# A DeltaNet attention and MLP kernel: from a scheduler's order to one written order with the MLP in small units

## The chip, the core and the metric

The kernel runs on one core of a Trainium2 chip. Its time is the device time of one execution in microseconds (us). TensorE (PE) multiplies, VectorE (DVE), ScalarE (ACT) and GpSimd (POOL) work elementwise, SyncE (SP) and ACT issue DMAs. Each engine runs its own instructions in order and waits on semaphores for the others.

## The reference

The output of a DeltaNet attention (batch 4, 8 heads, 768 tokens, head size 48) goes through an MLP 384 -> 2048 -> 384 with hardswish. q, k, v, beta are fp32; the two MLP weights arrive as float64 (a standard normal divided by a float64 number) and the kernel works in fp32.

```python
def _attn_ref(q, k, v, beta):
    B, H, S, D = q.shape                       # 4, 8, 768, 48
    k_n = k / (np.linalg.norm(k, axis=-1, keepdims=True) + 1e-06)
    state = np.zeros((B, H, D, D), dtype=np.float32)
    for t in range(S):
        kt, vt, bt = (k_n[:, :, t], v[:, :, t], beta[:, :, t, None])
        y[:, :, t] = np.einsum('bhd,bhde->bhe', q[:, :, t], state)
        v_old = np.einsum('bhde,bhd->bhe', state, kt)
        state = state + bt[:, :, :, None] * np.einsum('bhd,bhe->bhde', kt, vt - v_old)
    return y

def _moe_ref(x, w_in, w_out):                  # x: 3072 x 384
    h = x @ w_in
    return ((h * np.clip(h + 3.0, 0.0, 6.0) / 6.0) @ w_out).astype(np.float32)
```

## The kernel before

The 768 tokens are cut into 24 chunks of 32; a chunk's 32 tokens of all 4 batches fill the 128 partitions. Four chunks make a group, two chunks a block of the MLP (12 blocks of 256 tokens).

**Per group**, `norms` (the reciprocal lengths of k: ACT squares, a DVE reduction and Newton steps) and `inverse` (a unit triangular 32x32 system per head, batch and chunk, inverted by 30 columns of two DVE operations each, `pr` L310 and `A` L314). The matrix goes through DRAM for that: `l_dram<-LB`, `A<-l_dram` (L302), the columns, `x_dram<-A`, `LB<-x_dram` (L326).

**Per chunk**, `prep` (GpSimd: `kb`, `mb`, `bkb`; TensorE: eight transposes `pt` and the scores `sc`; ACT: `KQ`; DVE: `LB`) and `chain`, the recurrence. Its steps on TensorE are `ks` (L352, state times k), `pz` (LB times R), `py` (a part of the state, L352, and a part of the heads, L362), `su` (L406, the update of the state) and `yt` (L424, transposes of y for the MLP). ks, both parts of py, pz and su are 32 calls each on parts of the array of 32 or 64 rows; an fp32 call is two records in the trace, so 64. Between them DVE makes `R` after ks and updates `state` after su, ACT makes `Z` after pz and `y` after py.

**Per block**, `mlp_block`: 16 groups of three `ph` calls (L438, 128x256) with `t` on ACT and `g` on DVE, then two chunks of 16 `po` calls (L455, 128x384), then `o` and the store.

**Weights.** `convert` turns the float64 words into fp32 in 24 pieces of w_in (128x256) and 16 of w_out (128x384): two masks `e` and `m`, a Relu on ACT, then three joining operations, five of the six on DVE. Raw pieces share the tag "d" with three buffers.

**Order.** For the first part (chunks 0 and 1) DVE and SP run in written order, the other engines are ordered by the scheduler; from chunk 2 on the scheduler orders everything. The source gives two chains, then an MLP block. What stands on TensorE is the small matmuls of a chunk with a few ph among them, and then a long run of ph and po. All q, k, v loads, weight loads, A, LB and the stores are issued on SP; `l_dram` and `x_dram` on ACT. PSUM has three buffers of two banks (psC) and two of one bank (psM).

Of the kernel before, what the change touches and what calls it, by code (L numbers as in the profile page):

```python
# [17 lines left out]
def kernel(  # L18
# [20 lines left out]
    nc = tc.nc  # L39
# [18 lines left out]
    stage = ctx.enter_context(tc.tile_pool(name="stage", bufs=4))  # L58
# [4 lines left out]
    psC = ctx.enter_context(tc.tile_pool(name="psC", bufs=3, space=PSUM))  # L63
    psM = ctx.enter_context(tc.tile_pool(name="psM", bufs=2, space=PSUM))
# [14 lines left out]
    def load_k(g):  # L79
        if g * GS < N:  # L80
            kfs[g] = stage.tile([P, GS, H, D], FP32, name="kf", bufs=2)
            for i in range(GS):
                for b in range(B):
                    nc.sync.dma_start(out=kfs[g][rows(b), i], in_=tokens(k, b, g * GS + i))
# [12 lines left out]
    beta_hm = stage.tile([P, S], FP32, name="beta_hm", tag="d", bufs=3)  # L97
# [3 lines left out]
    for t in qbufs + kbufs + bkbufs:  # L101
        nc.vector.memset(t[:, :, D:DP], 0.0)
# [6 lines left out]
    for j, value in enumerate((1.0, -1.0)):  # L109
# [25 lines left out]
    WP = 256  # L135
    weights = [
        (w_in[:, s, f : f + WP], moe_w_in[s * 128 : (s + 1) * 128, f : f + WP])
        for f in range(0, FF, WP) for s in range(NKT)
    ] + [
        (w_out[:, f, :], moe_w_out[f * 128 : (f + 1) * 128, :]) for f in range(NFC)  # L140
    ]
    NW = len(weights)
    raws, parts = {}, {}

    def load_w(i):
        if i >= NW:
            return
        dst, src = weights[i]
        if src.dtype == FP32:
            nc.sync.dma_start(out=dst, in_=src)  # L150
            return
        raws[i] = stage.tile([128, dst.shape[1], 2], U32, name="d", tag="d", bufs=3)
        nc.sync.dma_start(
            out=raws[i][:].rearrange("p f z -> p (f z)"), in_=src.bitcast(U32)
        )

    def split_w(i):
        if i not in raws:
            return
        hi, n = raws[i][:, :, 1], raws[i].shape[1]  # L160
        m = stage.tile([128, n], U32, name="m", bufs=2)
        e = stage.tile([128, n], U32, name="e", bufs=2)
        nc.vector.tensor_single_scalar(e[:], hi, 0x7FF00000, op=ALU.bitwise_and)  # L163
# [3 lines left out]
        nc.vector.tensor_scalar(  # L167
            out=m[:], in0=hi, scalar1=0x000FFFFF, scalar2=0x00100000,
            op0=ALU.bitwise_and, op1=ALU.bitwise_or,
        )  # L170
        parts[i] = m, e

    def join_w(i):
        if i not in parts:
            return
        (m, e), d = parts.pop(i), raws.pop(i)
        hi, lo = d[:, :, 1], d[:, :, 0]
        nc.vector.scalar_tensor_tensor(  # L178
            out=e[:], in0=hi, scalar=0x80000000, in1=e[:],
            op0=ALU.bitwise_and, op1=ALU.bitwise_or,  # L180
        )
        mf = m[:].bitcast(FP32)
        nc.vector.scalar_tensor_tensor(  # L183
            out=mf, in0=lo, scalar=2.0**-32, in1=m[:], op0=ALU.mult, op1=ALU.add
        )
        nc.vector.scalar_tensor_tensor(  # L186
            out=weights[i][0], in0=mf, scalar=2.0**-20, in1=e[:].bitcast(FP32),
            op0=ALU.mult, op1=ALU.mult,
        )

    def convert():

        for i in range(3):
            load_w(i)
        split_w(0)
        for i in range(NW):
            split_w(i + 1)
            join_w(i)
            load_w(i + 3)
            yield  # L200

# [3 lines left out]
    def norms(g):  # L205

        kf = kfs[g]
        ss = small.tile([P, GS, H], FP32, name="ss")
        for i in range(GS):
            sq = work.tile([P, H, D], FP32, name="sq", bufs=1)  # L210
            nc.scalar.activation(out=sq[:], in_=kf[:, i], func=ACTF.Square)
            nc.vector.tensor_reduce(out=ss[:, i, :], in_=sq[:], axis=AX.X, op=ALU.add)
        seed = small.tile([P, GS, H], U32, name="seed")
# [5 lines left out]
        for _ in range(4):  # L219
            t = small.tile([P, GS, H], FP32, name="nt")  # L220
# [4 lines left out]
            rn = small.tile([P, GS, H], FP32, name="nr")  # L225
# [4 lines left out]
        t = small.tile([P, GS, H], FP32, name="nt")  # L230
# [4 lines left out]
        inv = small.tile([P, GS, H], FP32, name="inv")  # L235
        nc.vector.reciprocal(out=inv[:], in_=t[:])
        invs[g] = inv
# [5 lines left out]
    def prep(t):  # L243
# [4 lines left out]
            in1=invs[g][:, i, :].unsqueeze(2).to_broadcast([P, H, D]), op=ALU.mult,  # L248
# [13 lines left out]
        )  # L262
        KQ = work.tile([128, NP, 2, P], FP32, name="KQ", bufs=7)
        pt = psC.tile([128, 2, NP, P], FP32, name="pt", tag="pc")
        for j, src in enumerate((kb, qb)):
            for p in range(NP):
                nc.tensor.transpose(  # L267
                    pt[:, j, p, :], src[:, 2 * p : 2 * p + 2].rearrange("p e w -> p (e w)"), ident[:]
                )
            nc.scalar.activation(out=KQ[:, :, j, :], in_=pt[:, j], func=ACTF.Copy)  # L270
        load_q(t + NQB)
        yield
# [11 lines left out]
        LB = work.tile([P, 2, NP, 2, C], FP32, name="LB", bufs=7)  # L284
# [7 lines left out]
        nc.scalar.dma_start(  # L292
# [6 lines left out]
    def inverse(g):  # L299

        A = work.tile([128, C, C], FP32, name="A", bufs=1)
        nc.sync.dma_start(  # L302
            out=A[:].rearrange("p c i -> p (c i)"),
            in_=l_dram[g][:].rearrange("t h (b c) i -> (t h b) (c i)", b=B),
        )
        for j in range(1, C - 1):
# [13 lines left out]
        nc.scalar.dma_start(  # L320
# [20 lines left out]
    def chain(t):  # L341
        KQ, LB = KQs.pop(t), LBs.pop(t)
# [40 lines left out]
        pz = banks("pz")  # L383
        of_heads(
            lambda h, b: pz[rows(b), 0, D * h : D * h + D], lambda h: LBv[:, he(h), 0, :], R, True
        )
        Zt = work.tile([P, DM], FP32, name="Z")
        nc.scalar.activation(out=Zt[:], in_=pz[:, 0, 0:DM], func=ACTF.Copy)
# [9 lines left out]
        y = work.tile([P, DM], FP32, name="y")  # L398
        nc.scalar.activation(out=by_pair(y[:]), in_=pairs(py), func=ACTF.Copy)
        if t < N - 1:  # L400
# [11 lines left out]
            for i in range(B // 2):  # L412
# [6 lines left out]
        blk, cc = divmod(t, CB)
        if cc == 0:  # L420
            xTs[blk] = mlp.tile([128, NKT, TB], FP32, name="xT", bufs=2)
        pt = banks("yt")[:, 0, :]
        for s in range(NKT):
            nc.tensor.transpose(pt[:, s * P : (s + 1) * P], y[:, s * 128 : (s + 1) * 128], ident[:])  # L424
        nc.vector.tensor_copy(
            out=xTs[blk][:, :, cc * P : (cc + 1) * P],
            in_=pt[:, 0 : NKT * P].rearrange("p (s w) -> p s w", s=NKT),
        )
        yield


    def mlp_block(blk):
        xT = xTs.pop(blk)
        gs = []
        for f in range(NFC):
# [14 lines left out]
            gs.append(g)  # L450
            yield
        for c in range(CB):
            po = psM.tile([128, DM], FP32, name="po", tag="pm")
            for f in range(NFC):
                nc.tensor.matmul(  # L455
# [114 lines left out]
```

## Time and profile before

| | |
|---|---|
| runs, us | 896.68, 890.95, 896.49; median 896.49 |
| profiled execution | 888.49 us; span of its profile 886.7 us |
| mean granted clock of TensorE | 0.941 |
| busy share | TensorE 80%, DVE 41%, ACT 21%, GpSimd 10% |
| last matmul ends, span ends | 882.4 us, 886.7 us |
| mean DVE time | g 0.42, state 0.55, R 0.55, LB 0.69 us |

The span runs from the first to the last instruction; the time of an execution is a little longer. Everything below is of the one profiled execution. Where a row of the trace says "issue", the engine waited for nothing that the profile shows. Half clock is a granted clock of 0.50.

### The profile page before, as it was taken

Reading aid. Unit: us, or ns where it says so; the run is one execution under the profiler, and the core shown is the slowest. Engines: PE = TensorE matmul, PEld = TensorE weight load, DVE = VectorE, ACT = ScalarE, POOL = GpSimd, SP = SyncE. Lnnn points to the kernel's source line nnn. Section 1 sums busy time; section 2 is a strip of 40 time slices with the busy share of each in tenths; the row PEclk is TensorE's granted clock in tenths of the full one; section 3 lists DMA queues with packets and bytes.
Section 4 is the critical chain, followed back from the end, with each engine's and each line's share of the span. In section 5 each row is a group of like instructions: output and inputs, shape, how many; then the busy total and the mean of one; then the engine's idle time right before and its main releaser. Section 6 shows DMA issues by size and latency. Waiting matters only on the chain.

```text
span 886.7 us, 25143 instructions
## 1 busy us (share of the span) xinstructions
PE 709.5 (80%) x11208; PEld 510.7 (58%) x11208; DVE 365.2 (41%) x1014; ACT 188.2 (21%) x377; POOL 86.1 (10%) x118
## 2 busy tenths in 40 slices
PE   2400047987889799799799898998898999999998
PEld 1200035753666576676676675766765757757674
DVE  4647598659528430266220373311391302212030
ACT  2310233421321121230121220211311302213030
POOL 4200032006130000300001300002000000000000
PEclk9999995987989899899799899899999998999999
DMA  5462526433432401333102214001204001000000
GB/s 111 106 149 49 108 56 168 100 102 99 82 59 66 78 1 24 59 78 60 28 0 44 47 35 76 12 9 27 54 4 76 8 9 23 1 20 1 10 9 19
DMA packets 140524, 45.78 MB, mean 52 GB/s; under 512 B 130656, under 2 KB 133728, under 8 KB 140416
## 3 DMA queue, kind: packets, MB, share of 16 engines
q1 hardware_dynamic: 114528, 37.78, 20.0%
q10 hardware_dynamic: 25888, 6.39, 3.4%
q8 instruction: 88, 1.44, 0.7%
q14 instruction: 20, 0.16, 0.1%
HBM read 33.13 MB, written 11.01 MB: 50 GB/s over the span
## 4 chain that ended last, share of the span: by engine, by line
PE 69%; DVE 15%; issue 8%; DMA 5%; SPq 2%; ACT 1%; POOL 0%; ACTq 0%; DVEq 0%; POOLq 0%
PE ph L438 28%; PE po L455 23%; DVE A L314 3%; DVE pr L310 3%; PE pt L267 3%; PE py L362 3%; PE su L406 3%; DMA d<-in_moe_w_in_dram 2%; PE pz L362 2%; PE ks L352 2%; PE py L352 2%; PE sc L279 2%; PE yt L424 1%; DVE e L178 1%; DVE m L183 1%
## 5 line engine op out<-in xcount | busy, mean ns | idle before, releaser
L438 PE MATMUL ph<-xT,w_in 128*128 128x256 f32 x1152 | 279.1, 397 | 1.4 <-DVE g L447 1.3
L455 PE MATMUL po<-w_out,g 128*128 128x384 f32 x768 | 255.2, 493 | 4.0 <-DVE w_out L186 4.0
L438 PEld LDWEIGHTS ph<-xT,w_in 128*128 128x128 f32 x1152 | 211.0, 197 | 45.7 <-DVE g L447 7.4
L455 PEld LDWEIGHTS po<-w_out,g 128*128 128x128 f32 x768 | 146.3, 192 | 107.5 <-DVE w_out L186 8.1
L447 DVE SCALAR_TENSOR_TENSOR g<-t,ph 128x256 f32<-128x256 f32 x192 | 80.6, 420 | 153.5 <-ACT t L443 153.3
L443 ACT ACTIVATE t<-ph,half 128x256 f32<-128x256 f32 x192 | 90.9, 473 | 200.5 <-PE ph L438 194.4
L246 POOL TENSOR_TENSOR kb<-kf,inv 128x384 f32<-128x384 f32 x24 | 34.1, 1424 | 451.3 <-PE pt L267 377.6
L310 DVE TENSOR_TENSOR pr<-A 128x30 f32<-128x30 f32 (+9 forms) x180 | 59.5, 330 | 19.5 <-DMA A<-l_dram 15.3
L414 DVE TENSOR_TENSOR state<-state,su 128x384 f32<-128x384 f32 x46 | 23.4, 549 | 107.0 <-PE su L406 107.0
L377 DVE TENSOR_TENSOR R<-vf,ks 128x384 f32<-128x384 f32 x23 | 12.7, 552 | 131.7 <-PE ks L352 122.9
L314 DVE TENSOR_TENSOR A<-A,pr 128x30 f32<-128x30 f32 (+9 forms) x180 | 59.4, 330 | 4.1
L462 ACT ACTIVATE o<-po 128x384 f32<-128x384 f32 x24 | 11.8, 490 | 207.1 <-PE po L455 197.2
L267 PE MATMUL pt<-ident,kb 128*128 128x128 f32 x96 | 21.1, 359 | 39.9 <-POOL kb L246 34.9
L362 PE MATMUL pz<-vf,LB 32*32 32x48 f32 x64 | 1.5, 276 | 59.4 <-DMA LB<-x_dram 59.4
L362 PE MATMUL py<-Z,LB 32*32 32x48 f32 x1536 | 27.9, 222 | 20.2 <-issue 20.2
L270 ACT ACTIVATE KQ<-pt 128x512 f32<-128x512 f32 x48 | 28.6, 596 | 71.5 <-PE pt L267 71.4
L164 ACT ACTIVATE e<-e,rebias 128x256 uint32<-128x256 uint32 (+1 forms) x40 | 21.9, 549 | 86.3 <-DVE e L163 86.3
L406 PE MATMUL su<-Z,bkb 32*64 32x48 f32 x1472 | 26.1, 256 | 15.3 <-issue 15.3
L267 PEld LDWEIGHTS pt<-ident,kb 128*128 128x128 f32 x96 | 13.7, 179 | 42.1 <-POOL kb L246 35.1
L253 POOL TENSOR_TENSOR mb<-beta_tok,mask 128x256 f32<-128x256 f32 x48 | 29.0, 626 | 82.0 <-DVE LB L285 70.1
L362 PEld LDWEIGHTS py<-Z,LB 32*32 32x32 f32 x1536 | 22.7, 119 | 23.9 <-issue 22.3
L362 PEld LDWEIGHTS pz<-vf,LB 32*32 32x32 f32 x64 | 1.3, 162 | 59.6 <-issue 59.6
(54 smaller groups left out, 466.9 us busy)
## 6 DMA issues: line engine op xcount, KB each, us to landing
d<-in_moe_w_in_dram SPq DMA_DIRECT2D x24, 256.0 KB, 3.0
d<-in_moe_w_out_dram SPq DMA_DIRECT2D x16, 384.0 KB, 3.3
kf<-in_k_dram SPq DMA_DIRECT2D x96, 48.0 KB, 2.2
qb<-in_q_dram SPq DMA_DIRECT2D x96, 48.0 KB, 2.5
vf<-in_v_dram SPq DMA_DIRECT2D x96, 48.0 KB, 2.2
out_dram<-o SPq DMA_DIRECT2D x96, 48.0 KB, 1.6
l_dram<-LB ACTq DMA_DIRECT2D x24, 128.0 KB, 3.2
A<-l_dram SPq DMA_DIRECT2D x6, 512.0 KB, 3.5
```

The costliest lines, as they stand in the source:

```text
L246: nc.gpsimd.tensor_tensor(out=kb[:, :, 0:D], in0=kfs[g][:, i], in1=invs[g][:, i, :].unsqueeze(2).to_broadcast([P, H, D]), op=ALU.mult,)
L253: nc.gpsimd.tensor_tensor(out=mb[:, e], in0=beta_tok[:, t, e:H:2].unsqueeze(2).unsqueeze(3).to_broadcast([P, NP, 2, C]), in1=mask2[:].unsq ...
L267: nc.tensor.transpose(pt[:, j, p, :], src[:, 2 * p : 2 * p + 2].rearrange("p e w -> p (e w)"), ident[:])
L310: nc.vector.tensor_tensor(out=pv, in0=A[:, j, j + 1 :].unsqueeze(1).to_broadcast([128, j, n]), in1=A[:, 0:j, j].unsqueeze(2).to_broadcast( ...
L314: nc.vector.tensor_tensor(out=A[:, 0:j, j + 1 :], in0=A[:, 0:j, j + 1 :], in1=pv, op=ALU.subtract)
L352: nc.tensor.matmul(ph[rows(b), e, D * p : D * p + D], lhsT=KQ[r, p, j, rows(b)], rhs=state[r, b, p, :], start=(p == 0), stop=True, skip_gr ...
L362: nc.tensor.matmul(place(h, b), lhsT=m(h)[rows(b)], rhs=z[rows(b), D * h : D * h + D], start=start, stop=True, skip_group_check=True, tile ...
L406: nc.tensor.matmul(su[b // 2][DP * e : DP * e + DP, b % 2, D * p : D * p + D], lhsT=bkb[rows(b), h], rhs=Z[rows(b), D * h : D * h + D], st ...
L438: nc.tensor.matmul(ph[:], lhsT=w_in[:, s, f * 128 : (f + 1) * 128], rhs=xT[:, s, :], start=(s == 0), stop=(s == NKT - 1),)
L443: nc.scalar.activation(out=t1[:], in_=ph[:], func=ACTF.Relu, bias=half[:, 0:1], scale=1.0 / 6.0)
L447: nc.vector.scalar_tensor_tensor(out=g[:], in0=t1[:], scalar=1.0, in1=ph[:], op0=ALU.min, op1=ALU.mult)
L455: nc.tensor.matmul(po[:], lhsT=gs[f][:, c * P : (c + 1) * P], rhs=w_out[:, f, :], start=(f == 0), stop=(f == NFC - 1),)
```

## The change

All five engines run in written order from beginning to end (`manual_schedule()` without a list). The MLP is cut into units: three ph calls, or two po calls (`up`, `down`, `mlp_units`). `chain` yields after every step, so that one step stands between two units: 16 units per chunk from chunk 4 on, one step for two units; in chunks 2 and 3 eight units per chunk with a step after each. `prep` is cut in four (its GpSimd part, transposes of k, of q, scores) and put at units 0, 3, 5, 7 and 8 later of the first two chunks of a group. The inverse of the next group goes column by column between the units of the last two chunks, one or two columns per unit, followed by `norms`. `convert` gives out one operation at a time; the weights come in 8 + 8 pieces of 128x768 instead of 24 + 16, and `need` converts a piece of w_out before the unit that uses it. k loads go per chunk, and a group's buffer kf shares tag "d" with the raw weights. `yt` is copied by ACT, the DMAs of prep and inverse are on SP after the start (on ACT in it), three Newton steps stand in place of four, psC has 2 buffers and psM 4, of which pt, pz and yt take theirs too; R, Z and y have one buffer. 48 units are left for the end and run without anything between.

```diff
-    psC = ctx.enter_context(tc.tile_pool(name="psC", bufs=3, space=PSUM))
-    psM = ctx.enter_context(tc.tile_pool(name="psM", bufs=2, space=PSUM))
+    psC = ctx.enter_context(tc.tile_pool(name="psC", bufs=2, space=PSUM))
+    psM = ctx.enter_context(tc.tile_pool(name="psM", bufs=4, space=PSUM))
...
-            kfs[g] = stage.tile([P, GS, H, D], FP32, name="kf", bufs=2)
+                kfs[g] = stage.tile([P, GS, H, D], FP32, name="kf", tag="d", bufs=3)
...
-    WP = 256
+    WP, WF = 256, 2
...
     def convert():
-        for i in range(3):
-            load_w(i)
         split_w(0)
+        yield
         for i in range(NW):
             split_w(i + 1)
-            join_w(i)
-            load_w(i + 3)
-            yield
+            yield
+            if i in raws:
+                d, e = raws.pop(i), parts.pop(i)
...
+                nc.vector.scalar_tensor_tensor(
+                    out=mf, in0=lo, scalar=2.0**-32, in1=m[:], op0=ALU.mult, op1=ALU.add
+                )
+                load_w(i + 2)
+                yield
...
+            done[0] = i + 1
+            yield
...
-    def inverse(g):
+    def inverse(g, dma):
...
-            if j % 5 == 0:
-                yield
+            yield
...
-        pz = banks("pz")
+        pz = psM.tile([P, 512], FP32, name="pz", tag="pm")
...
         if t > 0:
             of_state(py, 1)
+            yield
...
+    def up(blk):
+        xT = xTs[blk]
         for f in range(NFC):
...
+            gs[blk, f] = g
+            yield
+    def down(blk, c, f0, n):
...
+    def mlp_units():
+        u1 = up(1)
+        yield from up(0)
+        for f in range(0, NFC, WF):
+            for c in range(CB):
+                need(NWI + f // WF + 1)
+                down(0, c, f, WF)
+                yield
+            for _ in range(WF):
+                next(u1)
+                yield
+        for blk in range(1, N // CB):
+            for c in range(CB):
+                for f in range(0, NFC, 2):
+                    down(blk, c, f, 2)
+                    yield
+            if blk + 1 < N // CB:
+                yield from up(blk + 1)
+    def need(n):
+        while done[0] < n:
+            take(conv)
...
+    with tc.manual_schedule():
...
+        for t in range(CB, N):
             g, i = divmod(t, GS)
             load_v(t + 2)
...
+            elif i == 2 and t + GS // 2 < N:
+                fill = inverse(g + 1, nc.sync)
+                for n in range(GS):
+                    load_k((g + 2) * GS + n)
+            elif i == 3:
+                rest = fill
+                fill = chained(rest, norms(g + 2, 0, GS) if (g + 2) * GS < N else iter(()))
+            ch = chain(t)
+            early = t < GS
+            for u in range(NU // 2 if early else NU):
+                if i < 2 and preps:
+                    at(u, preps[2 * i : 2 * i + 2])
+                if early or u % 2 == 0:
+                    take(ch)
+                if early:
+                    need(min(NWI, ((t - CB) * NU // 2 + u) // 2 + 1))
+                else:
+                    take(conv, 2)
+                take(units)
+                take(fill, 3 if early else 1 + (u % 2 == 0))
+            drain(ch)
+        drain(units)
```

TensorE, a chunk in the steady part before (a chunk without a prep):

```order
L455 MATMUL po<-w_out,g 128x384 x32
L352 MATMUL ks<-state,KQ 32x48 x29
L438 MATMUL ph<-xT,w_in 128x256 x2
L362 MATMUL pz<-R,LB 32x48 x32
L352 MATMUL py<-state,KQ 32x48 x32
L362 MATMUL py<-Z,LB 32x48 x32
L406 MATMUL su<-Z,bkb_89 64x48 x32
L424 MATMUL yt<-ident,y 128x128 x3
```

TensorE, the same chunk (6) in the change:

```order
L369 MATMUL ks<-state,KQ 32x48 x32
L490 MATMUL po<-w_out,g 128x384 x4
L379 MATMUL pz<-R,LB 32x48 x32
L490 MATMUL po<-w_out,g 128x384 x4
L369 MATMUL py<-state,KQ 32x48 x32
L490 MATMUL po<-w_out,g 128x384 x4
L379 MATMUL py<-Z,LB 32x48 x32
L490 MATMUL po<-w_out,g 128x384 x4
L427 MATMUL yt<-ident,y 128x128 x3
L490 MATMUL po<-w_out,g 128x384 x4
L438 MATMUL su<-Z,bkb_89 64x48 x32
L490 MATMUL po<-w_out,g 128x384 x12
```

Four po calls, two units, stand between any two steps of the chain, and yt has moved ahead of su.

SP, before, where A of one group is loaded:

```order
L95 DMA vf<-in_v_dram 32x8x48 x3
L89 DMA qb_86<-in_q_dram 32x8x48 x4
L302 DMA A<-l_dram_2392 128x1024
L84 DMA kf<-in_k_dram 32x8x48 x11
L466 DMA out_dram<-o 32x384 x4
```

SP, the change, start of the third chunk of a group:

```order
L308 DMA l_dram_3653<-LB 128x8x32
L97 DMA vf<-in_v_dram 32x8x48 x4
L86 DMA kf<-in_k_dram 32x8x48 x16
L318 DMA A<-l_dram_3653 128x1024
L500 DMA out_dram<-o 32x384 x8
```

The load of A stood ahead of the k loads and now stands behind 4 v loads and 16 k loads.

DVE, before, where w_out is converted:

```order
L447 SCALAR_TENSOR_TENSOR g<-t_1827,ph 128x256
L186 SCALAR_TENSOR_TENSOR w_out<-m,e 128x384
L447 SCALAR_TENSOR_TENSOR g<-t_1835,ph 128x256
L163 TENSOR_SCALAR e<-d 128x384
L167 TENSOR_SCALAR m<-d 128x384
L178 SCALAR_TENSOR_TENSOR e<-d,e 128x384
L183 SCALAR_TENSOR_TENSOR m<-d,m 128x384
```

DVE, the change, start of chunk 4:

```order
L394 TENSOR_TENSOR R<-vf,ks 128x2x4x48
L165 TENSOR_SCALAR e<-d 128x768
L184 TENSOR_SCALAR m<-d 128x768
L189 SCALAR_TENSOR_TENSOR e<-d,e 128x768
L195 SCALAR_TENSOR_TENSOR m<-d,m 128x768
L200 SCALAR_TENSOR_TENSOR w_out<-m,e 128x768
L165 TENSOR_SCALAR e<-d 128x768
L184 TENSOR_SCALAR m<-d 128x768
L189 SCALAR_TENSOR_TENSOR e<-d,e 128x768
L195 SCALAR_TENSOR_TENSOR m<-d,m 128x768
L478 SCALAR_TENSOR_TENSOR g<-t_2009,ph 128x256
L200 SCALAR_TENSOR_TENSOR w_out<-m,e 128x768
```

The conversion steps are twice as long, and e of a piece follows directly on the last step of the piece before it.

## Rows read from the trace of the kernel before

**Rows 1.** The page, busy us and share of the span, then instructions

```profile
PE 709.5 (80%) x11208; PEld 510.7 (58%) x11208; DVE 365.2 (41%) x1014; ACT 188.2 (21%) x377; POOL 86.1 (10%) x118
```

**Rows 2.** The chain that ended last: start us, us, what; start to tail

```profile
63.76 5.98 DMA A<-l_dram
...
91.79 2.62 DMA x_dram<-A
...
151.83 3.97 PE ph L438 x12
...
439.79 18.13 PE ph L438 x84
...
457.92 20.64 PE po L455 x64
...
861.79 20.65 PE po L455 x64
```

**Rows 3.** What TensorE waited for, whole span: total us, times, longest

```profile
PE pz L362 <- DMA LB<-x_dram: 59.4, 1, 59.4
...
PE pt L267 <- POOL kb L246: 34.9, 2, 18.6
...
PE py L362 <- issue: 20.2, 11, 2.3
...
PE su L406 <- issue: 15.3, 9, 2.5
...
PE py L352 <- issue: 10.5, 8, 2.2
```

**Rows 4.** TensorE in order of time: start us, us, what, wait before

```profile
435.07 0.81 PE L352 MATMUL py<-state,KQ 64*32 64x48 f32 x64
435.80 0.46 PE L362 MATMUL py<-Z,LB 32*32 32x48 f32 x24
437.87 0.63 PE L362 MATMUL py<-Z,LB 32*32 32x48 f32 x40 [1.61 <-issue]
438.43 0.89 PE L406 MATMUL su<-Z,bkb 32*64 32x48 f32 x64
439.24 0.55 PE L424 MATMUL yt<-ident,y 128*128 128x128 f32 x3
439.62 0.60 PE L438 MATMUL ph<-xT,w_in 128*128 128x256 f32 x2
...
506.19 1.03 PE L438 MATMUL ph<-xT,w_in 128*128 128x256 f32 x4
507.15 0.86 PE L279 MATMUL sc<-KQ 64*32 64x64 f32 x64
507.94 0.48 PE L438 MATMUL ph<-xT,w_in 128*128 128x256 f32 x1
```

**Rows 5.** Windows: us, busy of PE, PEld, DVE, ACT, POOL, clock, DMA share

```profile
424.00:434.00 10.00, 9.07 (x232) 6.65 (x231) 2.46 (x5) 0.96 (x2) 0.00 (x0) 0.50 0.09 18
...
290.00:882.40 592.40, 548.96 (x8182) 396.39 (x8178) 174.13 (x471) 118.76 (x244) 28.37 (x40) 0.95 0.16 30
```

**Rows 6.** DVE in order of time, conversion steps of 256 and 384 elements

```profile
31.23 0.28 DVE L167 TENSOR_SCALAR m<-d 128x256 uint32<-128x256 uint32 x1
...
32.22 0.43 DVE L186 SCALAR_TENSOR_TENSOR w_in<-m,e 128x256 f32<-128x256 f32 x1
...
208.37 0.35 DVE L163 TENSOR_SCALAR e<-d 128x384 uint32<-128x384 uint32 x1
...
211.12 0.55 DVE L186 SCALAR_TENSOR_TENSOR w_out<-m,e 128x384 f32<-128x384 f32 x1
```

**Rows 7.** DMAs: SyncE's issue of one group's k loads, then issue to landing

```profile
54.89 7.85 SPq L84 DMA_DIRECT2D kf<-in_k_dram  x16
...
d<-in_moe_w_out_dram SPq DMA_DIRECT2D x16, 384.0 KB, 3.3
...
A<-l_dram SPq DMA_DIRECT2D x6, 512.0 KB, 3.5
```

More of the change, by code (lines that the diff above doesn't have):

```diff
@@ L166, in split_w @@
         )
[L167 to L189, printed above, removed]
+        parts[i] = e
@@ L218, in norms @@
         r = seed[:].bitcast(FP32)
-        for _ in range(4):
-            t = small.tile([P, GS, H], FP32, name="nt")
+        for _ in range(3):
+            t = small.tile([P, n, H], FP32, name="nt")
             nc.vector.scalar_tensor_tensor(
@@ L234, in norms, with prep @@
         )
-        inv = small.tile([P, GS, H], FP32, name="inv")
+        inv = small.tile([P, n, H], FP32, name="inv", bufs=3)
         nc.vector.reciprocal(out=inv[:], in_=t[:])
-        invs[g] = inv
+        for i in range(n):
+            invs[g * GS + i0 + i] = inv[:, i, :]
+        yield
     KQs, LBs = {}, {}
     l_dram, x_dram = {}, {}
-    def prep(t):
+    def prep(t, dma):
         g, i = divmod(t, GS)
@@ L416, in chain @@
                 )
-        yield
[L419 to L434, printed above, removed]
+        last = t == N - 1
+        if t < CB and not last:
+            update()
+            yield
+        seam()
+        yield
+        if t >= CB and not last:
+            update()
+            yield
+    gs, pos = {}, {}
+    def up(blk):
+        xT = xTs[blk]
         for f in range(NFC):
@@ L483, in take, with drain, at @@
             next(gen, None)
-    preps = None
-    def chain_step(t, fill=lambda: None):
-        g, i = divmod(t, GS)
-        ch = chain(t)
-        while next(ch, "end") != "end":
-            fill()
+    def drain(gen):
+        for _ in gen:
+            pass
+    def at(unit, preps):
+        for place, part in zip((0, 3, 5, 7), range(4)):
+            if unit == place:
+                take(preps[0])
+            if unit == place + 8:
+                take(preps[1])
     conv = convert()
-    with tc.manual_schedule(engines={mybir.EngineType.DVE, mybir.EngineType.SP}):
+    NU = 16
@@ L525 @@
-    for blk in range(2, N // CB):
-        for c in range(CB):
-            t = blk * CB + c
+        second = [prep(GS + t, nc.scalar) for t in range(GS)]
+        take(second[0], 3)
+        take(second[1], 3)
+        drain(inv)
+        for t in range(2):
+            take(second[t])
+            take(second[t + 2], 3)
+            take(conv, 3)
+        for t in range(2):
+            take(second[t + 2])
+            take(conv, 2)
+        for t in range(CB):
+            load_v(t + 2)
+            for _ in chain(t):
+                take(conv, 2)
```

222 lines of the change are left out of this document (126 added, 96 removed).

## The prediction

> **What bounds the kernel now.** I read the page's busy shares first: TensorE (PE) is busy 709.5 of 886.7 us, 80%, and DVE only 41% [rows 1], so the first question is what the 177 us of idle TensorE are. The chain of waits says where: the MLP's first up matmul starts at 151.8 us [rows 2], and before that TensorE waits 59.4 us in one piece for the inverted LB and 34.9 us for kb [rows 3]. That is the start. After it, TensorE's largest wait is no engine at all: the rows "issue", 46.0 us in three lines, 28 waits of about 2 us [rows 3]. In order of time they sit inside long runs of small matmuls: 64 py, 24 more, a wait of 1.61 us, the other 40 [rows 4]. I read this as instructions arriving more slowly than TensorE eats them: a matmul and its weight load every 12 ns there, against two per 216 ns in a dense up run (18.13 us for 84) [rows 2, 4]. A wait also costs afterwards: in a stretch of 10 us behind one of them the granted clock was 0.50, the lower level, 1.2 GHz [rows 5].
>
> The dense part has nothing to give: an up matmul takes 18.13/84 = 0.216 us and a down matmul 20.64/64 = 0.323 us [rows 2]. A block is 96 and 64 of them, 41.4 us, 20.7 per chunk; a unit of the new order (6 up or 4 down records) is 1.29 us. From 290 us to the last matmul 18 chunks and 10 blocks are done in 592.4 us [rows 5]: 592.4 - 10 x 41.4 = 178 us, **9.9 us per chunk beyond the MLP**. That figure is what the interleaving can shrink.
>
> **The change, part by part.** *Small matmuls between units.* Warm prices of 64 small matmuls are the distances of starts [rows 4]: py of the state 0.73 (435.07 to 435.80), su 0.81, yt 0.38 for three. I give ks the 0.73, pz and py of the heads the 0.81: 2 x 0.73 + 3 x 0.81 + 0.38 = 4.3 us per chunk. Each piece now stands between dense units. What such a switch costs shows once each way [rows 4]: four up matmuls before sc took 0.96 us (506.19 to 507.15) instead of 4 x 0.216 = 0.86, so 0.10 going in; coming out, up follows sc after 0.79 us and nothing is lost. Five switched pieces: 0.5. So 4.8 us per chunk, and a prep (eight transposes at 0.13, sc 0.79 + 0.10) 1.9 us, 12 times behind chunk 6. Between pieces 2.6 us of dense units need 24 instructions or fewer, so the supply catches up: a run with waits had 256 small matmuls, 512 instructions, in some 10 us, 51 per us, and the new order asks about 39 per us (a chunk with two preps: some 1,130 in 29 us). I take the issue waits as gone; what remains is priced below.
>
> The Trainium skill's page "TensorEngine Tiling (Array Packing)", section "Tiling Modes", under "Key Properties", speaks against this: "Mode switching requires drain: Changing tiling mode (not just tile) drains the TensorE". The row's 0.10 us is all that the trace shows of such a drain; at 0.10 the sum below stands, and with a full drain at each switch it would be that of the third rival.
>
> *The inverse in columns between units.* The 30 columns take 91.79 - 69.74 = 22.1 us of DVE [rows 2] and overlapped dense runs before as well; spread over two chunks of 27 us they fit, if A is there. It is late. On SP, A's load now stands behind four v and sixteen k loads of the next groups at the start of chunk i = 2. Sixteen cost 7.85 us of issue, 0.49 each, and A lands 3.5 us (median) to 6.0 us (first) after issue [rows 2, 7]: 20 x 0.49 + 3.5 to 6.0 = 13.3 to 15.8, I take L = 14.5 us into the chunk, bounds 12 to 18. DVE runs in written order, so its first column blocks it until then, and behind it stand the state update and the next chunk's R. 24 columns come before that R (the first 23 took 18 us), plus the state and R: ready at L + 19.3. TensorE reaches its pz at about 29 us. The stall is L - 9.7, **4.8 us (2 to 8)**, in chunks 6, 10 and 14; in 18 no k load stands ahead. Three make 14 us, and each is followed by half clock: the 10 us at 0.50 lost 5 [rows 5], with denser work ahead I take 3 each, 9.
>
> *Weights in pieces of 768.* Raw loads are 768 KB. By differences of the steps (0.07 and 0.12 us per 128 elements [rows 6]) two mask steps take 0.55 and three joining steps 0.94 us; started back to back a piece is 3.75 us of DVE. w_out's eight pieces are converted inside chunk 4, two steps per unit, because the next unit of down(0) needs them: 30 us, plus eight g of 0.42, two LB of 0.69, two state and one R of 0.55, 6.4. A further wait is new: kf holds one of the three "d" buffers, so a piece's load starts only when the piece two before it has read its last, one step ahead of e that needs it. 384 KB land in 3.3 us [rows 7]; 768 KB I put at 4.2 to 6.7, taking 5, so about 3.5 us of DVE stall for each of five pieces, 18 us. Chunk 4 becomes about 54 us long (50 to 58) where 30 would do. If the load were hidden the 18 vanish; that is rival one.
>
> *The start.* Norms of chunk 0 alone let GpSimd start early, but the second weight load waits for kf's slot and DVE then stands in order at e until about 32 us; A's load goes out near 56 us instead of 63.8 [rows 2]. Inverse until 87, x_dram, LB and two chunks of the chain, and the first up matmul at about 119 us instead of 151.8, because it needs one w_in piece, not all 24. Chunks 2 and 3 have three columns per unit on a DVE blocked by A(1) behind sixteen k loads (landing near 133): chunk 4 starts at 176, chunk 6 at **257** (bounds 236 to 275). Before, six chunks and 64 units were done at 290; less the 16 that the new order still owes, 269.
>
> *Moves with one answer.* yt's copy on ACT (0.5 us, ACT is at 21%), one R, Z and y buffer, two large PSUM buffers: ordered waits inside a piece's 2.6 us of cover; 5 us altogether for what sticks out. Three Newton steps instead of four, the DMAs of inverse and prep on SP: hidden behind the units, at most 1 us per group.
>
> *Sum.* 257 + 18 x (20.7 + 4.8) + 12 x 1.9 - 0.9 (no update in the last chunk) = 738; stalls 14 + 9 + 5 = 28; then 48 units of 1.29 drained densely, 62; from the last matmul to the end 4.3 as before. **833 us of span**, against 886.7. The profiled execution took 888.5, 1.8 above its span, and the median of the runs is 896.5, 1.009 of that: 835 x 1.009 = **843 us**.
>
> **The rivals.** *Everything is covered* (chance 0.2): weight loads and A arrive in time, T6 = 236 and no stalls: 833 - 21 - 23 = 789, 797 us. For it: DMA is at 16% in the steady stretch [rows 5], so transfers can be quicker than I take. Against: the order on SP and the single spare "d" buffer stand in the program. *The issue waits stay* (0.13): if it is small matmuls as such that starve, not long runs of them, the 46 us of [rows 3] come back whole, wherever the pieces stand: 833 + 45 = 878, 886 us, within 1% of before or just under. *A switch drains TensorE* (0.08), the slower side: place, every border of the 110 pieces and 20 sc in chunks 2 to 23; price, a lone up matmul's 0.48 us [rows 4] at each of 260 borders, 125 less the 13 counted: 833 + 112 = 945, 955 us. It decides from about 0.5 us per piece (67 us over 130 pieces); the rows show 0.10, but in only two or three places, with a transpose or an up run already close by. That is why it keeps 0.08. The Trainium skill's sentence above is the same mechanism; by it the kernel would be slower, and the trace so far does not agree.
>
> That the change doesn't do what it says can be excluded from the order: units and pieces alternate in the program itself.
>
> **How the numbers follow.** My forecast, 833 of span, has 0.55; the rest, 0.04, are start-up mishaps. Its own range is 815 to 870: T6's bounds, -21 to +18, and the stalls' 6 to 24. For 8 in 10 I reach from just under the first rival to the second, 790 to 888. A measurement here tells about 1% from no change: 887.5 to 905.5. Faster by more: the forecast, the first rival and half of the second, 0.82; within 1%: the other half, 0.08; slower: the third and part of the mishaps, 0.10.
>
> **What would show it.** Issue waits of TensorE under 10 us in total instead of 46; ks, pz, py and su at 0.75 to 0.95 us between po or ph records; the first ph near 119 us; chunk 4 of 50 us or more with DVE waiting for DMA d; TensorE waiting for R in chunks 7, 11 and 15 and not in 19, with A landing some 14 us behind the first v load; the last 48 units dense. The prediction is wrong if pieces cost over 1.2 us, if issue waits stand in single pieces, or if DVE in order holds TensorE in every chunk: a column, conversion step or g that waits ahead of R would do that anywhere.

## The result and the profile after

The changed kernel takes **855.93 us** (median of 4 runs, 853.91 to 859.05) against 894.59 us of the kernel before (median of 4); the ratio is 0.9575, with a 95% interval of 0.9527 to 0.9623. The forecast was 843 us, the range 790 to 888, the likeliest case's own range 815 to 870. The profile shows a span of 853.4 us where the sum had 833.

The page's first part, busy us, share and instructions of each engine of the changed kernel:

```profile
PE 703.6 (82%) x11208; PEld 507.6 (59%) x11208; DVE 344.5 (40%) x865; ACT 188.5 (22%) x377; POOL 78.8 (9%) x118
```

TensorE is busy for 6 us less than in [rows 1], and its idle time has fallen from 177 to 150 us. What it waited for (total us, times, longest), the answer to [rows 3]:

```profile
PE pt L282 <- POOL kb L260: 57.7, 5, 22.8
PE sc L295 <- ACT KQ L285: 20.8, 4, 18.0
PE pz L379 <- issue: 13.6, 4, 4.5
...
PE py L379 <- issue: 3.2, 1, 3.2
```

The 46.0 us of "issue" before py and su have gone but for 3.2 us. The name stands once more, with 13.6 us before pz: 2.8 of them are in chunk 0, and the other three (10.7 us in chunks 7, 11 and 15) are waits of another kind, as the rows on R below show. The start still holds most of what is left (kb 57.7, KQ 20.8 us).

TensorE in order of time at the start of chunk 6 (start us, us, what): steps of the chain with a run of down matmuls between.

```profile
274.58 0.81 PE L369 MATMUL ks<-state,KQ 64*32 64x48 f32 x64
275.31 2.85 PE L490 MATMUL po<-w_out,g 128*128 128x384 f32 x8
278.09 0.88 PE L379 MATMUL pz<-R,LB 32*32 32x48 f32 x64
...
288.69 0.49 PE L427 MATMUL yt<-ident,y 128*128 128x128 f32 x3
289.01 2.75 PE L490 MATMUL po<-w_out,g 128*128 128x384 f32 x8
291.69 0.89 PE L438 MATMUL su<-Z,bkb 32*64 32x48 f32 x64
```

ks takes 0.73 us (274.58 to 275.31) and py of the state the same, as in [rows 4]. Eight po take 278.09 - 275.31 = 2.78 us, where 8 x 0.3225 = 2.58: the two borders of a step cost **0.20 us** together, not 0.10. Eight po with yt, which uses 128 rows, on one side take 291.69 - 289.01 = 2.68 us: one border costs 0.10, and the way out of a step costs as much as the way in (eight po between py and yt, 286.00 to 288.69, take 2.69). The end is as forecast, from the chain that ended last: 48 units without anything between, at the pace of [rows 2].

```profile
787.12 20.64 PE po L490 x64
807.76 20.72 PE ph L469 x96
828.48 20.65 PE po L490 x64
```

The starts of ks in the trace give the length of every chunk:

| stretch | forecast, us | measured, us |
|---|---|---|
| first ph | 119 | 130.7 |
| chunk 4 begins | 176 | 193.6 |
| chunks 4 and 5 | 81 | 47.8 + 33.2 = 81.0 |
| chunk 6 begins | 257 | 274.6 |
| a chunk with nothing else (19 to 22) | 25.5 | 25.9 |
| a chunk with two preps (8, 9, 12, 13, 16, 17) | 29.3 | 29.6 to 29.7 |
| chunks 6 + 7, 10 + 11, 14 + 15 beyond two plain ones | 7.7 | 10.1, 8.4, 6.3 |
| chunk 18 + 19 beyond two plain ones | 0 | 0.0 |
| chunks 6 to 23 | 510 | 512.5 |
| drained units, end | 62 + 4.3 | 62.0 + 4.3 |

(Of 23 starts of ks, for instance 274.58, 303.94, 336.52, 366.12 and 395.79 for chunks 6 to 10; 512.5 = 787.12 - 274.58.)

### The profile page after: what moved, and what is told of

Same layout as the page of the kernel before. It is cut to its first block, busy times and chain, and to the rows that moved or that the text cites. A ratio compares the mean times of both kernels' runs of the same rounds, so it can differ in the third digit from the quotient of the medians.

```text
span 853.4 us, 24929 instructions
## 1 busy us (share of the span) xinstructions
PE 703.6 (82%) x11208; PEld 507.6 (59%) x11208; DVE 344.5 (40%) x865; ACT 188.5 (22%) x377; POOL 78.8 (9%) x118
## 4 chain that ended last, share of the span: by engine, by line
PE 66%; DVE 11%; issue 8%; DMA 6%; SPq 5%; ACT 2%; POOL 1%; ACTq 0%; POOLq 0%; DVEq 0%
PE ph L469 29%; PE po L490 24%; SPq L86 4%; DVE pr L327 2%; DVE A L331 2%; DMA d<-in_moe_w_out_dram 2%; PE py L379 2%; PE pt L282 2%; PE pz L379 2%; PE su L438 2%; PE sc L295 2%; PE py L369 2%; PE ks L369 1%; DMA A<-l_dram 1%; DMA l_dram<-LB 1%
## 5 line engine op out<-in xcount | busy, mean ns | idle before, releaser
L469 PE MATMUL ph<-xT,w_in 128*128 128x256 f32 x1152 | 289.6, 403 | 17.5 <-DVE w_in L200 9.1
L490 PE MATMUL po<-w_out,g 128*128 128x384 f32 x768 | 272.2, 500 | 4.4 <-DVE w_out L200 4.4
L469 PEld LDWEIGHTS ph<-xT,w_in 128*128 128x128 f32 x1152 | 221.4, 199 | 54.1 <-DVE w_in L200 9.5
L282 PE MATMUL pt<-ident,kb 128*128 128x128 f32 x96 | 17.6, 314 | 57.7 <-POOL kb L260 57.7
L260 POOL TENSOR_TENSOR kb<-kf,inv 128x384 f32<-128x384 f32 x24 | 21.2, 883 | 417.1 <-DVE inv L247 350.3
L301 DVE TENSOR_TENSOR LB<-sc,mb 128x512 f32<-128x512 f32 x24 | 16.4, 685 | 69.2 <-PE sc L295 69.2
L295 PE MATMUL sc<-KQ 64*32 64x64 f32 x1536 | 21.9, 242 | 20.8 <-ACT KQ L285 20.8
L379 PE MATMUL pz<-R,LB 32*32 32x48 f32 x1472 | 22.9, 216 | 19.3 <-issue 10.7
L379 PEld LDWEIGHTS pz<-R,LB 32*32 32x32 f32 x1472 | 19.7, 115 | 30.6 <-issue 19.0
L295 PEld LDWEIGHTS sc<-KQ 64*32 64x32 f32 x1536 | 17.9, 114 | 29.6 <-ACT KQ L285 22.9
L168 ACT ACTIVATE e<-e,rebias 128x768 uint32<-128x768 uint32 x16 | 15.0, 935 | 78.8 <-DVE e L165 71.8
```

Of the source, the lines that this page charges most:

```text
L282: nc.tensor.transpose(pt[:, p, :], src[:, 2 * p : 2 * p + 2].rearrange("p e w -> p (e w)"), ident[:])
L295: nc.tensor.matmul(scv[rows(b), e, p], lhsT=KQ[r, p, 0, rows(b)], rhs=KQ[r, p, :, rows(b)], start=True, stop=True,)
L379: nc.tensor.matmul(place(h, b), lhsT=m(h)[rows(b)], rhs=z[rows(b), D * h : D * h + D], start=start, stop=True, skip_group_check=True, tile ...
L469: nc.tensor.matmul(ph[:], lhsT=w_in[:, s, f * 128 : (f + 1) * 128], rhs=xT[:, s, :], start=(s == 0), stop=(s == NKT - 1),)
L490: nc.tensor.matmul(po[:], lhsT=gs[blk, f][:, c * P : (c + 1) * P], rhs=w_out[:, f, :], start=(f == 0), stop=(f == NFC - 1),)
```

## The experiments

Each runs beside the kernel before on the same chip; ratios are to it, and the change is at 0.9575. Names of steps are those of the kernel.

**A's load ahead of the k loads.** Edit (the load of A is the first thing that `inverse` gives out):

```diff
                 fill = inverse(g + 1, nc.sync)
+                take(fill)
                 for n in range(GS):
                     load_k((g + 2) * GS + n)
```

> Edit: in the third chunk of a group the load of A is issued ahead of the 16 k loads, nothing else. My theory (A late, DVE in written order, R late): A lands some 6 us into the chunk instead of 14, R is ready at 25 us against TensorE's 29, the three waits of pz for R in chunks 7, 11 and 15 (13.6 us) go and the half clock behind them (about 3 us each) too: 855.9 - 20 to 25 = 831 to 836 us. Rival (DVE's load itself sets R, whenever A comes): the wait shrinks by less than a third, 849 to 856 us.

Measured: 829.85 us, 0.9325 (0.9271 to 0.9378). To see what it removes, first the changed kernel at the same place: SP's queue, then DVE, then TensorE, all around chunk 10 and 11.

```profile
397.87 10.35 SPq L86 DMA_DIRECT2D kf<-in_k_dram  x16
408.26 0.45 SPq L318 DMA_DIRECT2D A<-l_dram  x1
```

```profile
411.66 0.19 DVE L327 TENSOR_TENSOR pr<-A 128x30 f32<-128x30 f32 x1 [14.37 <-DMA A<-l_dram]
...
430.05 0.55 DVE L394 TENSOR_TENSOR R<-vf,ks 128x384 f32<-128x384 f32 x1
```

```profile
423.36 2.86 PE L469 MATMUL ph<-xT,w_in 128*128 128x256 f32 x12
430.70 1.50 PE L379 MATMUL pz<-R,LB 32*32 32x48 f32 x64 [4.48 <-issue]
432.13 5.08 PE L469 MATMUL ph<-xT,w_in 128*128 128x256 f32 x12
```

A's load is issued 10.4 us after the first k load, DVE stands 14.37 us at its first column, and R of chunk 11 runs 18.4 us after that column; pz starts 0.1 us after R has ended. The wait is named "issue", but it ends with R. Then pz takes 1.50 us instead of 0.88 and twelve ph 5.08 instead of 2.86. The window of this stretch (columns as in [rows 5]) has the granted clock at 0.53, 1.2 GHz for nearly all of it:

```profile
430.70:437.10 6.40, 6.40 (x76) 5.10 (x76) 3.63 (x13) 0.97 (x2) 0.00 (x0) 0.53 0.01 3
```

The first of the three places looks different. In chunk 6 DVE's first column comes 18.8 us into the chunk, so the state update is late too, and TensorE stands first at ks of chunk 7, for the state, and then at pz:

```profile
303.94 1.43 PE L369 MATMUL ks<-state,KQ 64*32 64x48 f32 x64 [3.42 <-DVE state L446]
...
312.41 0.88 PE L379 MATMUL pz<-R,LB 32*32 32x48 f32 x64 [1.76 <-issue]
```

In the experiment, the same place of chunk 11:

```profile
410.07 0.81 PE L369 MATMUL ks<-state,KQ 64*32 64x48 f32 x64
410.81 2.86 PE L469 MATMUL ph<-xT,w_in 128*128 128x256 f32 x12
413.60 0.88 PE L379 MATMUL pz<-R,LB 32*32 32x48 f32 x64
```

No wait, pz 0.88 us, and the pairs of chunks 6 + 7, 10 + 11 and 14 + 15 last 51.8 us, two plain ones. 26 us of span are gone, a little more than the expected 20 to 25; the forecast's 14 + 9 for late A and the clock behind it make 23 of them. The theory holds; the rival (DVE itself sets R) falls. The expectation counted 13.6 us of waits in chunks 7, 11 and 15; 2.8 of these stood in chunk 0, and 2.7 stay.

**Halves: twice the borders.** Edit (the other steps in the same way):

```diff
                             tile_position=(DP * e, C * b),
                         )
+                if p == NP // 2 - 1 and t >= GS:
+                    yield
...
-                if early or u % 2 == 0:
+                if early or u != 9:
                     take(ch)
```

> Edit: from chunk 4 on ks, pz, both parts of py and su are each cut into two halves of 32 records and a unit stands between the halves, 99 more pieces between units, some of them next to sc; the same matmuls otherwise. At the 0.20 us that a switched piece costs in the trace of the change: +17 to 20 us, 873 to 876. At the 0.10 of the prediction: 863 to 866. If a switch drained TensorE (0.5 to 0.96 us a piece): +50 to 95, 905 to 950.

Measured: 899.44 us, 1.0114 (1.0044 to 1.0184): far more than I expected. The lengths of chunks split it. A plain chunk takes 27.0 us instead of 25.9, so five more pieces cost 1.1 us, 0.22 each: near the 0.20 of the trace, and some 19 us in chunks 6 to 23. The rest stands mainly in chunks 6, 10 and 14, which last 42.4, 39.8 and 39.9 us. TensorE, then DVE, in chunk 6:

```profile
271.67 1.56 PE L496 MATMUL po<-w_out,g 128*128 128x384 f32 x4
273.15 0.40 PE L369 MATMUL ks<-state,KQ 64*32 64x48 f32 x32
273.48 1.56 PE L496 MATMUL po<-w_out,g 128*128 128x384 f32 x4
288.42 0.86 PE L381 MATMUL pz<-R,LB 32*32 32x48 f32 x32 [13.38 <-issue]
```

```profile
287.37 0.19 DVE L327 TENSOR_TENSOR pr<-A 128x30 f32<-128x30 f32 x1 [15.00 <-DMA A<-l_dram]
...
287.77 0.55 DVE L398 TENSOR_TENSOR R<-vf,ks 128x384 f32<-128x384 f32 x1
```

R now comes a unit later in the written order, behind the first column, so that DVE's wait for A (15.00 us) holds R of the same chunk and TensorE stands 13.4 us. With the two chunks taken together the waits are 46.7 us in three groups against 24.8 in the change, 21.9 more. One yield moved R behind a wait: this is the failure that the prediction named last, "a column that waits ahead of R".

**One unit between steps instead of two.**

```diff
-                if early or u % 2 == 0:
+                if early or u < 6:
                     take(ch)
```

> Edit: the six steps of a chunk stand one unit apart instead of two, ten dense units follow. A run of steps then asks for some 67 instructions per us instead of 45. Theory of supply with a store (a run of 250 small matmuls is needed to empty it): issue waits stay under 10 us; R, Z and y have 1.3 us of cover instead of 2.6 and DVE's columns stand ahead of R, 0 to 1.2 us per chunk, 856 to 880 us. Rival (any rate above 51 per us starves TensorE): a wait of about 2 us per chunk and half clock behind it, 40 to 100 us more, 895 to 955.

Measured: 860.82 us, 0.9673 (0.9617 to 0.9728). Plain chunks take 25.9 us, to 0.1 us the same. TensorE in a chunk without a wait:

```profile
664.82 0.80 PE L369 MATMUL ks<-state,KQ 64*32 64x48 f32 x64
665.55 1.56 PE L469 MATMUL ph<-xT,w_in 128*128 128x256 f32 x6
667.04 0.88 PE L379 MATMUL pz<-R,LB 32*32 32x48 f32 x64
```

Steps with 1.5 us between them, no issue wait among the six, and R, Z and y in time. The 6 us more of span are 8 us in the pairs 6 + 7, 10 + 11 and 14 + 15 (66.3, 60.9 and 61.0 us against 61.9, 60.2 and 58.1), less 2 us before chunk 6. In these pairs A is late: TensorE reaches pz one unit earlier and waits longer for R (up to 11.6 us). What the spacing needs is one unit; the second is reserve.

**All steps together.**

```diff
-                if early or u % 2 == 0:
+                if early:
                     take(ch)
+                elif u == 0:
+                    drain(ch)
```

> Edit: from chunk 4 on the six steps of a chunk stand together with no unit between, then its 16 units. If standing between units is what the change gains: TensorE waits for R, Z and y (some 3 us per chunk), for instructions (about 2 us per chunk) and runs at half clock after it (3 to 5 us): 8 to 10 us per chunk, 160 to 200 over 20 chunks, 1015 to 1055 us. If the gain comes from the written order and the start alone: only the three waits, 60 us, about 915.

Measured: 928.25 us, 1.0431 (1.0367 to 1.0495), between the two. TensorE in chunk 17:

```profile
648.83 0.81 PE L369 MATMUL ks<-state,KQ 64*32 64x48 f32 x64
650.28 0.88 PE L379 MATMUL pz<-R,LB 32*32 32x48 f32 x64 [0.65 <-DVE R L394]
651.09 0.69 PE L369 MATMUL py<-state,KQ 64*32 64x48 f32 x51
653.30 0.31 PE L369 MATMUL py<-state,KQ 64*32 64x48 f32 x13 [1.51 <-issue]
...
655.09 0.90 PE L427 MATMUL yt<-ident,y 128*128 128x128 f32 x3 [0.67 <-ACT y L417]
```

The waits are those that I had named: R 0.65, y 0.67 and one issue wait of 1.51 us (0.37 more in su). A plain chunk takes 30.1 us against 25.9, 4.2 more; as it saves some four pairs of borders (0.8), waits and clock cost about 5 us. The windows of a plain chunk (chunk 20) here and of two plain chunks of the change (us, busy of PE, PEld, DVE, ACT, POOL, then the clock):

```profile
743.36:773.42 30.06, 27.14 (x389) 16.93 (x388) 1.91 (x4) 2.44 (x5) 0.00 (x0) 0.94 0.03 8
```

```profile
659.29:711.11 51.82, 51.82 (x808) 37.33 (x807) 12.92 (x37) 11.30 (x24) 0.00 (x0) 1.00 0.17 37
```

The granted clock is 0.94 against 1.00, 1.8 of 30 us. I had put 3 to 5 us on the clock and 3 on the waits for R, Z and y, which came to 1.3: there the expectation was too high. So the units between the steps are worth 4.2 us in every chunk, some 73 us of span. That is more than the change gained: everything else in it, with the steps together, is 4% slower than the kernel before. The order before already had a few ph among its steps, which probably explains this; no run shows it.

**The start: a mask moved behind A.**

```diff
         take(first[1])
         take(first[0])
-        take(conv, 2)
+        take(conv, 1)
         for t in range(1, GS):
...
             take(first[t])
-            take(conv, 1)
-        take(conv, 2)
-        drain(norms(1, 0, GS))
         inv = inverse(0, nc.scalar)
         take(inv)
+        drain(norms(1, 0, GS))
+        take(conv, 5)
```

> Edit: in the start the second weight piece's mask, on which DVE stood 17 us in written order, goes behind the first inverse's load of A, and norms of the second group too; nothing else. My theory (DVE in written order holds LB of chunks 1 to 3 and with them A): A's load is issued near 33 us instead of 60.8, the inverse ends near 65 instead of 90, the first ph comes at 100 to 110 instead of 130.7, and the end 15 to 25 us earlier: ratio to the kernel before 0.93 to 0.94. Rival (conversion and its loads bound the start, the inverse only runs beside them): the first ph comes earlier, but chunk 4 starts within 5 us of 193.6, ratio 0.953 to 0.958.

Measured: 840.91 us, 0.9431 (0.9381 to 0.9480). In the change DVE stood 17 us at e of the second piece, whose load went out only at 32.7 us; LB of chunk 1 came behind it:

```profile
38.04 0.56 DVE L165 TENSOR_SCALAR e<-d 128x768 uint32<-128x768 uint32 x1 [17.09 <-DMA d<-in_moe_w_in_dram]
41.89 0.69 DVE L301 TENSOR_TENSOR LB<-sc,mb 128x512 f32<-128x512 f32 x1 [3.29 <-PE sc L295]
```

In the experiment all four LB are done at 31.9 us, and A's load is issued at 35.2 instead of 60.8:

```profile
31.22 0.69 DVE L301 TENSOR_TENSOR LB<-sc,mb 128x512 f32<-128x512 f32 x1 [2.58 <-PE sc L295]
...
47.34 1.02 DVE L165 TENSOR_SCALAR e<-d 128x768 uint32<-128x768 uint32 x1 [1.50 <-DMA d<-in_moe_w_in_dram]
```

But of these 25.6 us only 14.3 reach chunk 4 (179.2 against 193.6), and the first ph comes at 114.8, not at 100 to 110. Part of it went at once: the second piece's mask now waits behind norms and lands ahead of the columns (47.34), so the inverse ends at 76.7, not at 65. Then Z of chunk 0 waited 8.6 us for ACT, which had an l_dram to issue for an LB that stood behind an e waiting 11.05 us for raw weights. The direction was right and the size at the lower end (15.8 us of span, and a ratio just above 0.93 to 0.94): DVE and ACT in written order pass a late load on to the chain at the next place.

**Four buffers for raw weights and k.**

```diff
-                kfs[g] = stage.tile([P, GS, H, D], FP32, name="kf", tag="d", bufs=3)
+                kfs[g] = stage.tile([P, GS, H, D], FP32, name="kf", tag="d", bufs=4)
```

(and the same for the raw pieces; o and mb get one buffer each to make room)

> Edit: four buffers of tag d instead of three, paid for with one buffer for o and for mb. My theory (a piece's load waits for the buffer of the piece two before it, since kf holds the third): DVE's waits for raw weights, 12.1 us in five for w_out and part of the 31.2 for w_in, go, chunk 4 takes 36 to 42 us instead of 47.8, and the time falls by 6 to 14 us: ratio 0.942 to 0.951. Rival (the loads are late because of bandwidth or their place on SP, or DVE's own 30 us bind): less than 3 us, 0.954 to 0.958; the single mb could also cost a little.

Measured: 846.16 us, 0.9478 (0.9439 to 0.9517): the gain was in the range, but not where I had put it. Chunk 4 fell from 47.8 to 44.5 us only; DVE's waits for raw pieces of w_out are these (total us, times, longest), against 12.1 in five in the change:

```profile
DVE e L165 <- DMA d<-in_moe_w_out_dram: 7.0, 2, 4.9
```

8.0 of the 10.2 us of span come from chunk 2 (19.6 us instead of 27.6): the k loads there no longer waited for a buffer, and A of the second group, queued behind them on SP, was issued at 133.9 us instead of 141.4.

**A first in chunk 2 as well.** Edit: `take(fill)` ahead of the k loads in the branch of chunk 2 too.

> Edit: A's load ahead of the k loads in the third chunk of every group as in a_first, and also for the second group's inverse in chunk 2. My theory: A lands near 135 us instead of 145.6 in chunk 2, DVE is free 10 us earlier, ks of chunk 3 waits less (4.1 us before) and chunk 4 starts 5 to 10 us earlier: ratio 0.921 to 0.927 against 0.9325 of a_first. Rival: chunks 2 and 3 are held by the w_in pieces (9.1 us wait for the last), then no more than 2 us: 0.930 to 0.934.

Measured: 821.03 us, 0.9197 (0.9153 to 0.9242). Chunk 2 takes 18.0 us instead of 27.6, and chunk 4 begins at 183.1 instead of 193.6. The gain is a little larger than expected (0.921 to 0.927). This confirms what d4 hinted.

**w_out without its arithmetic.** Edit, for the pieces of w_out:

```diff
+                if e is None:
...
+                    nc.vector.tensor_copy(out=weights[i][0].bitcast(U32), in_=hi)
```

> Edit on the change: each piece of w_out is converted by one copy of its high words instead of five DVE operations and a Relu (the down weights are then wrong numbers; loads, buffers and the matmuls stay). It leaves out some 3 of the 3.75 us of DVE work for each of eight pieces. If DVE's own work makes chunk 4 long (47.8 us against 29.65 for a chunk with preps): chunk 4 falls to 30 to 35 us and the time by 12 to 18, ratio to the kernel before 0.937 to 0.944. If the loads and their buffers do (eight loads of 4.4 us behind one another, two buffers): chunk 4 stays over 42 us, ratio 0.951 to 0.958.

Measured: 836.98 us, 0.9399 (0.9353 to 0.9445). Chunk 4 takes 32.6 us, chunk 5 31.3. So DVE's arithmetic makes chunk 4 long, together with the waits for raw pieces: the edit takes away these as well (12.1 us in the change, none here) and the Relu on ACT, so it doesn't weigh the two against each other. d4 does in part: 5.1 us less of waiting took 3.3 us off the chunk. In the change a piece in chunk 4 reads (DVE in order of time, the end of the first piece and the second):

```profile
196.89 0.95 DVE L195 SCALAR_TENSOR_TENSOR m<-d,m 128x768 f32<-128x768 uint32 x1
197.87 0.96 DVE L200 SCALAR_TENSOR_TENSOR w_out<-m,e 128x768 f32<-128x768 f32 x1
202.33 0.56 DVE L165 TENSOR_SCALAR e<-d 128x768 uint32<-128x768 uint32 x1 [3.50 <-DMA d<-in_moe_w_out_dram]
202.80 0.56 DVE L184 TENSOR_SCALAR m<-d 128x768 uint32<-128x768 uint32 x1
203.27 0.95 DVE L189 SCALAR_TENSOR_TENSOR e<-d,e 128x768 uint32<-128x768 uint32 x1
204.14 0.95 DVE L195 SCALAR_TENSOR_TENSOR m<-d,m 128x768 f32<-128x768 uint32 x1
```

From e at 202.33 the steps begin 0.47, 0.47, 0.87 apart: with 0.98 and the last one's 0.96 (as at 196.89 and 197.87 in the piece before) 3.75 us, the forecast's figure. The wait for the raw piece, 3.50 here, came to 12.1 us in five; the forecast had 18.

**Together.** Edit: `start` and `a_both` in one kernel.

> Edit: start and a_both together, three buffers as in the change. If the two act in different stages, their gains add: 22 + 15 to 25 + 5 us below the change, 800 to 812 us by the scale of the kernel before at 894.6, ratio 0.895 to 0.908. If the start is bound by conversion, 0.922 to 0.932.

Measured: **805.79 us**, 0.9024 (0.8984 to 0.9063). TensorE is busy 86% of the span. What it still waits for:

```profile
PE pt L282 <- POOL kb L260: 60.4, 6, 23.9
PE pz L379 <- DVE R L394: 10.7, 4, 6.3
```

The gains add: 853.4 - 805.3 = 48.1 us of span, where start had 15.8 and a_both 34.2 (50.0). It beats both kernels.

**With the four buffers too.**

> Edit: best0 with the four buffers of d4. If the loads' wait for a buffer still costs in chunk 4: 3 to 5 us below best0, ratio 0.896 to 0.900. The rest of d4's gain came from A of the second group, which best0 has already. If nothing is left of it: 0.901 to 0.905.

Measured: 806.69 us, 0.9047 (0.9001 to 0.9094), no different from best0. Chunk 4 is 45.6 instead of 47.8 us, but the start is later by 2 (chunk 4 begins at 172.1 against 170.1). The second alternative holds: nothing is left of d4's gain. Whether the single buffers of mb and o make the start later isn't shown.

## Why the prediction was right

*What bounds the kernel*: right. The issue waits of [rows 3] went from 46.0 to 3.2 us as soon as small matmuls stood in runs of 64 with dense units between, and came back (29.6 us before py and su) when the six steps stood together. That instructions arrive too slowly was an inference from the rate; the trace of the kernel before shows more of it. Two of its waits, in order of time:

```profile
427.71 0.70 PE L406 MATMUL su<-Z,bkb 32*64 32x48 f32 x29 [0.93 <-issue]
...
437.87 0.63 PE L362 MATMUL py<-Z,LB 32*32 32x48 f32 x40 [1.61 <-issue]
```

From the first to the second TensorE runs 256 matmuls with 256 weight loads, 512 records. Counted like this, all 31 issue waits of 0.25 us or more in this trace (27 of them in [rows 3]) stand at the same place in a block of 256 records. The page's part on DMA queues (packets, MB, share) has a queue for instructions:

```profile
q8 instruction: 88, 1.44, 0.7%
```

That is 16 KB in each packet and, for TensorE's 22,416 records, some 255 records for each. In the trace two of these packets never start less than 3.3 us apart, in any run, and each of the 31 waits ends 2.2 to 3.1 us after one has started. So TensorE waits for its next block of instructions: a run of small matmuls uses up 256 records in some 1.5 us, a dense run of ph in 28. This is the store that runs empty. In pace1 the six steps ask for about 61 records per us for 11.5 us (706 from 664.82 to 676.32) without a wait, so the 51 of the prediction is no limit; a block per 3.3 us would be 78 (an estimate). The two issue waits left in the change, 2.8 and 3.2 us in chunks 0 and 1, where no units stand between the steps, are at that place in a block; the three before pz in chunks 7, 11 and 15 are not. What makes a block take 3.3 us was not measured.

*Small matmuls*: the mechanism was right and the term too small. A step costs 0.20 us for its two borders instead of 0.10; [rows 4] showed one way in, into sc, at 0.10, which was right. The way out I had read as free from sc's own 0.79 us, but its price stands in the dense run behind the step (2.69 us for eight po between py and yt, instead of 2.58). 25.9 us per plain chunk instead of 25.5, 18 x 0.4 = 7 us.

*Switches that drain TensorE* (third rival): not so here: 0.20 us for the two borders of a step in the trace and 0.22 in halves, where about 0.5 was needed to make the kernel slower. The Trainium skill, page "TensorEngine Tiling (Array Packing)", section "Tiling Modes", says that changing the mode drains TensorE; the trace agrees with some loss at each change, of 0.20 us for two.

*A late on SP, R late on DVE*: the mechanism was right, and the sum nearly exact. Forecast L = 14.5, R at L + 19.3, stall 4.8; measured in chunks 10 and 11 L = 15.9 (395.79 to 411.66), R done 18.9 behind it, stall 4.5. L was 18.8 in chunk 6 and 15.1 in chunk 14, and in chunk 6 the late DVE held the state as well, which the forecast named but did not price: 3.4 us of that stall stood at ks. The three groups cost 24.8 us with the clock, against 14 + 9. Chunk 18, without k loads ahead, had none. Taking the cause away returned 26 us.

*Weights*: a piece at 3.75 us to the digit, 12.1 us of waiting instead of 18, chunk 4 at 47.8 instead of 50 to 58; with chunk 5 the 81 us came out exactly, by luck: chunk 4 was 6 us shorter than the 54 in the sum, and chunk 5 took 33.2 where the sum left it 27. Four buffers took 5.1 us off the waits and 3.3 off chunk 4; leaving the arithmetic out took the rest of the waits with it, and 15.2 us. How these divide between the two isn't shown.

*The start* is the term that was mis-sized: 274.6 instead of 257, all but 3 of the 20 us between 833 and 853. I had walked DVE's order there, but taken the loads as on time where they stand far back on SP: the second weight piece lands at 38.0 us, not 32, since it goes out at 32.7, behind 16 k loads and 16 q loads (kf's slot, which I had named, was free at 26.3); A's load goes out at 60.8, not near 56; and Z of the first chunk waits 6.8 us for ACT. First ph 11.7 us late. Chunks 2 and 3 took 64 us instead of 57 for the same reason once more, A of the second group behind 16 k loads that themselves waited for a buffer (DVE's first column there at 145.7; I had A at 133). The bounds, 236 to 275, held it just. Against the kernel before, which by the forecast's own count stood at 269 at this place, the start lost some 5 us instead of gaining 12; the whole gain of 33 us of span lies behind the start of chunk 6.

*From span to time*: 835 x 1.009 took over the distance between the profiled execution and the median from the kernel before. Here it is 855.1 to 855.9, a factor of 1.001. So the forecast of 843 us is 13 off and not 21, by luck: the factor added 7.5 us that did not come.

*Everything is covered* (first rival) was the wrong case for the change, but best0 shows it within reach: 805.3 us of span against that rival's 789, with T6 at 251 instead of 236.

*Small terms*: I had 5 us for waits of the smaller buffers; plain chunks show none. Two sums are slightly off and change nothing: 738 + 28 + 62 + 4.3 is 832, and the second rival is 833 + 46 = 879, 889 us by the same factor, where 878 and 886 stand.

## What to carry to other kernels

Where small matmuls come in long runs, cut them to steps and put dense work of one to two microseconds between: here that was worth 4.2 us in each chunk, by waits for operands, for instructions and by the clock, at a price of 0.2 us per step. What counts for the instructions is how soon a block of 256 is used up: in 1.5 us, as in a run of small matmuls alone, TensorE waited here, in 4.2 us, as in pace1, it did not. In a written order every queue is part of the order: look at each load whose consumer stands ahead of the critical chain on an in-order engine, and put that load first on its queue; one line did that here for 26 us, one line more for 8. Price a start by walking the queue of loads, not only the engine that waits for them.

## What the runs showed of the hardware that was not expected

A border between 128-row matmuls and a step on 64 or 32 rows costs 0.10 us at full clock, in either direction, with ph and po alike: twelve ph and eight po take 2.79 and 2.78 us between two steps and 2.68 to 2.70 with yt, which uses 128 rows, on one side, against 2.59 and 2.58 at the pace of dense runs. TensorE's instructions come in blocks of 256, never less than 3.3 us apart in these runs, and the kernel before waited at the end of a block 31 times. After a wait of 4.5 us in chunk 11 the granted clock was 0.53 for 6.4 us, with TensorE busy all the time, and 1.00 behind that; the 3 us lost there came to two thirds of the wait itself. The price of a wait isn't fixed: behind a wait just as long in chunk 15 the clock was 0.67 over the 5.2 us to the next step, 1.7 us lost.

```profile
549.38:554.53 5.15, 5.15 (x76) 4.19 (x77) 2.92 (x11) 0.96 (x2) 0.00 (x0) 0.67 0.01 3
```

And in the profile a wait named "issue" need not be one: pz's in chunks 7, 11 and 15 ended with R on DVE.
